# Weight transposes at other places in a queue of tile transposes, one tile's statistics sooner, and another order of V tiles and fusion groups

## The chip, the cores and the metric

The kernel runs on one core of a Trainium2 chip. The metric is the device time of one execution in microseconds; below it is the median of three runs. All times in the text are microseconds, and times inside an execution count from the start of its span.

## The reference

x has 2048 rows (tokens) of 640 values in bf16. Each row is normalised (mean and variance over its 640 values), and the result xn feeds two branches. Their sum and x itself make the output.

- Branch A is linear attention with 32 heads of 20 values. q, k, v = xn @ wqkv. A small matrix per head (w_phi, 20 x 20) turns q and k into features: softmax(p) and softmax(-p) side by side, p = q w_phi or k w_phi. Per head kv = sum over tokens of phi_k v, z = sum over tokens of phi_k; the output is (phi_q kv) / (phi_q z + 1e-6), then @ wo.
- Branch B is a gated unit with 1536 hidden values: (silu(xn w1) * (xn w3)) @ w2.

```python
xn = _layernorm(x)
return x + _A_ref(xn, A_wqkv, A_w_phi, A_wo) + _B_ref(xn, B_w1, B_w3, B_w2)
```

## The kernel before

The rows are cut into 16 tiles of 128 tokens. TensorE contracts over the partition dimension, so it wants xn transposed: xnT holds 5 chunks of 128 of the 640 values, by token. All of the program's order is written out by hand (a manual schedule): within an engine, instructions run in the order in which the text emits them, and engines wait for each other by semaphores.

The work has three stages. The first, which the change touches, normalises and transposes all 16 tiles, computes v of all tiles, and folds w_phi into the weights of k. The second makes phi_k tile by tile and accumulates kv, with units of the gated branch between. The third makes phi_q, the quotient and the two output products tile by tile.

The pieces of the first stage, by the names that the text uses:

- `ld_tiles(t, n)` (lines 128 to 132) loads n tiles of x, `ld_glu(f0, f1)` (114) columns of w1 and w3. All DMAs are issued by SyncE (SP), one after the other, and their data run on the same 16 DMA engines.
- `stats(t, n)` (563) takes the statistics of n tiles: bn_stats and bn_aggr on VectorE (203, 204), then the inverse square root by a short chain on GpSimd (212 to 242).
- `lx(t, n)` (570) normalises the tiles in place, on VectorE (255) or, for tiles 12 and 13, on ScalarE (250).
- `T(t)` (260) transposes a normalised tile into xnT. Tiles 0 to 3 go over TensorE. From tile 4 on it is a DMA transpose from SBUF to SBUF, issued by SP (265).
- `ldT(wkT, 1, d)` (120 to 124) is a DMA transpose of rows 128 d to 128 d + 127 of k's weights out of DRAM, 128 x 640 values. There are five pieces. The text calls them K0 to K4. The five of q's weights follow them.
- `V(t)` (300) is v of tile t: ten matmuls of 128 x 320 (290) that read xnT of the tile, and two copies from PSUM to SBUF on ScalarE (303).
- `FB(d)` (580) is one fusion group: six small matmuls that multiply piece Kd by the block-diagonal w_phi (371), and two copies of the result into wkphi[:, d] on ScalarE (380). It needs Kd.
- `unit()` (588) is a unit of the gated branch for tokens 0 to 511, five matmuls of gate and five of up (387); calling what it returns (g0() to g4()) makes the product on VectorE (400, 403).
- `phi_blocks()` (361) builds the block-diagonal w_phi on VectorE.

The stage ends with `V(12), FB(0), FB(1), V(13), FB(2), FB(3), V(14), FB(4), V(15)` (672). The second stage starts with the product pk of tile 0 (`by_token`, 283 to 298): it goes over the five chunks c = 0 to 4 with two matmuls each, and chunk c reads wkphi[:, c].

PSUM has six banks of one kind, taken in turn, two by each V and by each odd FB; an even FB takes a pair of its own.

Of the kernel before, what the change touches and what calls it, by code (L numbers as in the profile page):

```python
# [12 lines left out]
def kernel(  # L13
# [55 lines left out]
    def bank(name, dt=f32):  # L69
        n = 512 if dt == f32 else 1024  # L70
        return psum.tile([P, n], dt, name=name, tag="bank")

    def pair(name):
        return psum2.tile([P, 2, 512], f32, name=name, tag="pair")
# [21 lines left out]
    wkT, wqT, wv = w_nat[:, 0], w_nat[:, 1], w_nat[:, 2]  # L96
# [11 lines left out]
    def ld(dst, src):  # L108
        nc.sync.dma_start(out=dst, in_=src)
# [4 lines left out]
    def ld_glu(f0, f1):  # L114
        for w, src in ((w1, B_w1), (w3, B_w3)):
            ld(w[:, :, f0:f1], src[:, f0:f1].rearrange("(c p) f -> p c f", p=P))

    wps = one.tile([P, KD, Dh], bf, name="wps")
    with tc.manual_schedule():
        def ldT(dst, i, d):  # L120
            rows = slice(d * P, (d + 1) * P)
            nc.sync.dma_start_transpose(  # L122
                out=dst[:, :, rows], in_=A_wqkv[rows, i * D : (i + 1) * D]
            )
# [3 lines left out]
        def ld_tiles(t, n):  # L128
            ld(
                xin[:, (t // 4) % 3, t % 4 : t % 4 + n],  # L130
                x2[t * P : (t + n) * P, :].rearrange("(t p) d -> p t d", p=P),
            )
# [66 lines left out]
        def ln_stats(t):  # L199
            xt = xin[:, (t // 4) % 3, t % 4, :]  # L200
            st = work.tile([P, 2, 6], f32, name="st")
            for i in range(2):
                nc.vector.bn_stats(out=st[:, i, :], in_=xt[:, i * HD : (i + 1) * HD])  # L203
            nc.vector.bn_aggr(out=mv[:, t, :], in_=st[:])
# [5 lines left out]
        def ln_pow(t, n):  # L210
            r = slice(t, t + n)
            nc.gpsimd.tensor_scalar(
                out=ve[:, r], in0=mv[:, r, 1], scalar1=EPS, scalar2=None, op0=ALU.add
            )
            nc.gpsimd.tensor_tensor(out=ry[:, r], in0=ve[:, r], in1=mhalf[:, 0:n], op=ALU.pow)  # L215

        def ln_newton(t, n):


            r = slice(t, t + n)  # L220
            eng = nc.vector if t < BY_DMA else nc.gpsimd
            if n == 1:
                eng.tensor_scalar(
                    out=rstd[:, r], in0=ry[:, r], scalar1=ve[:, r], scalar2=ry[:, r],
                    op0=ALU.mult, op1=ALU.mult,
                )
            else:
                eng.tensor_mul(out=rstd[:, r], in0=ry[:, r], in1=ry[:, r])
                eng.tensor_mul(out=rstd[:, r], in0=rstd[:, r], in1=ve[:, r])
            if t < BY_DMA:  # L230
                nc.vector.scalar_tensor_tensor(
                    out=rstd[:, r], in0=rstd[:, r], scalar=-3.0, in1=ry[:, r],
                    op0=ALU.add, op1=ALU.mult,
                )
            else:
                nc.gpsimd.tensor_scalar(
                    out=rstd[:, r], in0=rstd[:, r], scalar1=-0.5, scalar2=1.5,
                    op0=ALU.mult, op1=ALU.add,
                )
                nc.gpsimd.tensor_mul(out=rstd[:, r], in0=rstd[:, r], in1=ry[:, r])  # L240
            if t in BY_ACT:
                nc.gpsimd.tensor_scalar(
                    out=shift[:, r], in0=mv[:, r, 0], scalar1=rstd[:, r], scalar2=-1.0,
                    op0=ALU.mult, op1=ALU.mult,
                )

        def ln_x(t):
            xt = xin[:, (t // 4) % 3, t % 4, :]
            if t in BY_ACT:
                nc.scalar.activation(  # L250
                    out=xt, in_=xt, func=AF.Identity,
                    scale=rstd[:, t : t + 1], bias=shift[:, t : t + 1],
                )
                return
            nc.vector.tensor_scalar(  # L255
                out=xt, in0=xt, scalar1=mv[:, t, 0:1], scalar2=rstd[:, t : t + 1],
                op0=ALU.subtract, op1=ALU.mult,
            )
# [102 lines left out]
        def phi_blocks():  # L361
            nc.vector.tensor_mul(
                out=wphi[:],
                in0=wps[:, :, None, :].to_broadcast([P, KD, 8, Dh]),
                in1=mask[:, :, :, None].to_broadcast([P, KD, 8, Dh]),
            )

        def fuse(dst, wT, d, ps):

            for b, c, h0, h1 in PARTS:  # L370
                nc.tensor.matmul(  # L371
                    ps[b][:, Dh * (h0 - 16 * b) : Dh * (h1 - 16 * b)],
                    wT[:, c, d * P : (d + 1) * P],
                    wphi[:, c, h0 - 6 * c : h1 - 6 * c, :],
                    start=((b, c) in ((0, 0), (1, 2))),
                    stop=((b, c) in ((0, 2), (1, 4))),
                    skip_group_check=True,
                )
            for b in range(2):
                nc.scalar.copy(out=dst[:, d, b * HD : (b + 1) * HD], in_=ps[b][:, 0:HD])  # L380
# [182 lines left out]
        def stats(t0, n):  # L563
            for t in range(t0, t0 + n):
                ln_stats(t)
            ln_pow(t0, n)
            if t0 >= BY_DMA:
                ln_newton(t0, n)

        def lx(t0, n):  # L570
            if t0 < BY_DMA:
                ln_newton(t0, n)
            for t in range(t0, t0 + n):
                ln_x(t)
# [3 lines left out]
        T, V = x_transposed, v_unit  # L578

        def FB(d):  # L580
            if d % 2:
                ps = [bank("pf"), bank("pf")]
            else:
                both = pair("pf")
                ps = [both[:, 0], both[:, 1]]
            fuse(wkphi, wkT, d, ps)

        def unit():
            return glu_unit(*glu.pop(0))
# [25 lines left out]
        T(3)  # L615
        ld_tiles(12, 2)
        ld_tiles(14, 2)
        V(2)
        V(3)
        stats(4, 2)  # L620
# [5 lines left out]
        g0()  # L626
        lx(6, 2)
        T(6, 7)
        ldT(wkT, 1, 0)
        stats(8, 1)  # L630
        stats(9, 1)
        g2 = unit()
# [7 lines left out]
        lx(9, 1)  # L640
        T(9)
        ld_glu(512, 768)
        ldT(wkT, 1, 1)
        V(7)
        stats(10, 2)
        g3 = unit()
        stats(12, 1)
        lx(10, 2)
        T(10, 11)
        ldT(wkT, 1, 2)  # L650
        stats(13, 1)
        V(8)
        g3()
        stats(14, 2)
        lx(12, 1)
        T(12)
        V(9)
        ldT(wkT, 1, 3)
        g4 = unit()
        lx(13, 1)  # L660
        T(13)
        V(10)
        ldT(wkT, 1, 4)
        phi_blocks()
        g4()
        lx(14, 2)
        T(14, 15)
        V(11)
        ld_glu(768, F)
        for d in range(KD):  # L670
            ldT(wqT, 0, d)
        V(12), FB(0), FB(1), V(13), FB(2), FB(3), V(14), FB(4), V(15)


        acc = pair("pkv")
# [105 lines left out]
```

## Time and profile before

| | |
|---|---|
| median of 3 runs | 273.03 (272.68 to 273.33) |
| the profiled execution | 273.45 |
| its span, first to last instruction | 271.6 |
| TensorE busy | 263.9 (97% of the span) |
| VectorE, ScalarE, GpSimd busy | 189.9, 109.6, 97.1 |
| granted TensorE clock | 1.0 throughout |

The span is what the profile shows; some 1.85 of the execution lie outside it. Busy times of matmuls are modelled: a matmul's shown length holds a tail in which the next one already runs, so two matmuls in a row overlap in the view. A row of the timeline merges equal instructions that follow each other; its first number is the start of the first one. "SPq" rows are DMAs being issued, and the length is the time for which the issue held SyncE, not the transfer. The DMA view has the time from issue to landing.

### The profile page before, as it was taken

To read this page: it belongs to the slowest core of one execution; us is meant where nothing else is said; L and a number is where in the kernel's file an instruction comes from. 1 tells how busy PE (TensorE), PEld (TensorE's weight loads), DVE (VectorE), ACT (ScalarE), POOL (GpSimd) and SP (SyncE) were. 2 spreads that over 40 slices of the span, in tenths; PEclk is the share of its full clock that TensorE was granted. 3 is DMA by queue.
4 is the path that set the end of the run, shared out by engine and by line. 5 is a ranking of instruction groups with operands and counts; after the bars stand their busy time and mean duration, and the time that the engine had idled before them with its cause. 6 is when DMAs were issued, how large, how long until landed. Compare 5 with 4: busy or idle time off the path is not lost.

```text
span 271.6 us, 5174 instructions
## 1 busy us (share of the span) xinstructions
PE 263.9 (97%) x1972; PEld 166.7 (61%) x1990; DVE 189.9 (70%) x349; ACT 109.6 (40%) x258; POOL 97.1 (36%) x104
## 2 busy tenths in 40 slices
PE   7899989999999999999999999999999999999995
PEld 7646566555555555555554455677777777777773
DVE  5999740887766777777778778877676677777341
ACT  6734657534555553455564455422222222221000
POOL 5254630454333333344433312333334444433000
PEclk9999999999999999999999999999999999999999
DMA  6997858950000000000000944346775765576931
GB/s 209 321 202 140 189 116 236 200 138 0 2 0 2 0 0 2 0 5 0 0 2 5 279 113 77 78 107 143 120 162 129 135 143 126 126 137 142 148 102 54
DMA packets 64380, 27.80 MB, mean 102 GB/s; under 512 B 50144, under 2 KB 64352, under 8 KB 64352
## 3 DMA queue, kind: packets, MB, share of 16 engines
q1 hardware_dynamic: 64352, 27.43, 45.6%
q8 instruction: 17, 0.28, 0.4%
q14 instruction: 11, 0.09, 0.1%
HBM read 12.81 MB, written 2.62 MB: 57 GB/s over the span
## 4 chain that ended last, share of the span: by engine, by line
PE 92%; DVE 2%; DMA 2%; SPq 1%; issue 1%; POOL 1%; ACT 0%
PE acc L505 27%; PE up L387 19%; PE gp L387 19%; PE pq L290 8%; PE pk L290 8%; PE pv L290 6%; PE pkv L413 2%; PE pr L442 2%; DVE st L203 1%; DMA xnT<-reg_h 1%; DMA reg_h<-in_A_x_dram 1%; PE pf L371 1%; SPq L122 0%; POOL ry L215 0%; DVE reg_h L255 0%
## 5 line engine op out<-in xcount | busy, mean ns | idle before, releaser
L353 POOL TENSOR_TENSOR phi<-phi,rk 128x1320 bf16<-128x1320 bf16 x32 | 77.2, 2412 | 136.8 <-DVE rk L352 132.8
L350 DVE TENSOR_REDUCE sk<-phi 128x66 f32<-128x1320 bf16 x32 | 48.9, 1528 | 41.7 <-ACT phi L317 40.7
L387 PEld LDWEIGHTS <-w 128*128 128x128 bf16 x480 | 45.5, 98 | 50.6
L387 PE MATMUL up<-xnT,w 128*128 128x512 bf16 x237 | 59.5, 379 | 0.3
L290 PEld LDWEIGHTS <-xnT 128*128 128x128 bf16 x480 | 45.4, 98 | 23.0 <-DMA xnT<-reg_h 2.4
L387 PE MATMUL gp<-xnT,w 128*128 128x512 bf16 x225 | 58.5, 378 | 0.7
L505 PE MATMUL acc<-reg_v,reg_h 128*128 128x320 bf16 (+2 forms) x384 | 54.9, 299 | 0.0
L317 ACT ACTIVATE phi<-pq 128x360 bf16<-128x360 f32 (+1 forms) x64 | 23.3, 451 | 59.2 <-POOL phi L353 53.8
L505 PEld LDWEIGHTS <-reg_h 128*128 128x128 bf16 x384 | 37.3, 98 | 14.4
L395 ACT ACTIVATE th<-gp 128x512 f32<-128x512 f32 x48 | 28.8, 600 | 34.6 <-PE gp L387 30.6
L403 DVE SCALAR_TENSOR_TENSOR reg_h<-gs,up 128x512 bf16<-128x512 bf16 x48 | 33.0, 688 | 5.3 <-PE up L387 0.5
L317 ACT ACTIVATE phi<-pk 128x360 bf16<-128x360 f32 (+1 forms) x64 | 23.3, 451 | 24.7 <-PE pk L290 15.7
L400 DVE SCALAR_TENSOR_TENSOR gs<-th,gp 128x512 bf16<-128x512 f32 x48 | 31.6, 658 | 0.0
L514 DVE TENSOR_TENSOR res<-acc,xr 128x320 bf16<-128x320 f32 (+2 forms) x32 | 14.3, 487 | 21.5 <-PE acc L505 21.5
L290 PE MATMUL pk<-wkphi,xnT 128*128 128x360 bf16 (+2 forms) x160 | 24.6, 300 | 0.0
L290 PE MATMUL pq<-wqphi,xnT 128*128 128x360 bf16 (+2 forms) x160 | 24.6, 299 | 0.0
L505 PE MATMUL acc<-reg_w,reg_v 128*128 128x320 bf16 (+2 forms) x160 | 24.5, 299 | 0.0
L290 PE MATMUL pv<-reg_w,xnT 128*128 128x320 bf16 x160 | 23.2, 299 | 1.3 <-DMA xnT<-reg_h 1.3
L352 DVE RECIPROCAL rk<-sk 128x66 f32<-128x66 f32 x32 | 18.1, 566 | 3.2
L505 PEld LDWEIGHTS <-reg_v 128*128 128x128 bf16 x160 | 15.7, 98 | 6.1
L303 ACT CAST reg_v<-pv 128x320 bf16<-128x320 f32 x32 | 12.1, 430 | 11.4 <-PE pv L290 11.4
L203 DVE BATCH_NORM_STATS2 st<-reg_h 128x6 f32<-128x320 bf16 x32 | 13.7, 469 | 2.1 <-DMA reg_h<-in_A_x_dram 2.1
(62 smaller groups left out, 135.2 us busy)
## 6 DMA issues: line engine op xcount, KB each, us to landing
xr<-in_A_x_dram SPq DMA_DIRECT2D x16, 160.0 KB, 2.5
out_dram<-res SPq DMA_DIRECT2D x15, 160.0 KB, 1.8
reg_h<-in_A_x_dram SPq DMA_DIRECT2D x7, 320.0 KB, 5.8
w<-in_B_w_dram SPq DMA_DIRECT2D x6, 320.0 KB, 5.7
w<-in_B_w_dram SPq DMA_DIRECT2D x2, 960.0 KB, 6.8
reg_v<-in_B_w_dram SPq DMA_DIRECT2D x3, 640.0 KB, 6.1
reg_w<-in_A_wo_dram SPq DMA_DIRECT2D x1, 800.0 KB, 6.3
reg_w<-in_A_wqkv_dram SPq DMA_DIRECT2D x2, 320.0 KB, 4.5
```

What stands on the lines that cost most here:

```text
L203: nc.vector.bn_stats(out=st[:, i, :], in_=xt[:, i * HD : (i + 1) * HD])
L290: nc.tensor.matmul(ps[i][:, 0 : b - a], xnT[:, c, cols], w[:, c, a:b], start=(c == 0), stop=(c == KD - 1), skip_group_check=True,)
L317: nc.scalar.activation(out=to[g], in_=p.rearrange("p (c f) -> p c f", f=60), func=AF.Exp, scale=1.0 - 2.0 * g,)
L350: nc.vector.reduce_sum(out=sk[:], in_=rows, axis=AX.X)
L352: nc.vector.reciprocal(out=rk[:], in_=sk[:])
L353: nc.gpsimd.tensor_mul(out=rows, in0=rows, in1=rk[:, :, :, None].to_broadcast([P, 2 * NCH, 3, Dh]))
L387: nc.tensor.matmul(ps[:], w[:, c, fi * P : (fi + 1) * P], xnT[:, c, sc * 512 : (sc + 1) * 512], start=(c == 0), stop=(c == KD - 1),)
L395: nc.scalar.activation(out=th[:], in_=gp[:], func=AF.Tanh, scale=0.5)
L400: nc.vector.scalar_tensor_tensor(out=gs[:], in0=th[:], scalar=1.0, in1=gp[:], op0=ALU.add, op1=ALU.mult)
L403: nc.vector.scalar_tensor_tensor(out=hT[:, 4 * sc : 4 * sc + 4, fi, :], in0=gs[:].rearrange("p (t s) -> p t s", t=4), scalar=0.5, in1=up[: ...
L505: nc.tensor.matmul(ps[:, 0 : b - a], rows[j][0], rows[j][1][:, a:b], start=(j == 0), stop=(j == len(rows) - 1),)
L514: nc.vector.tensor_tensor(out=res[:, a:b], in0=ps[:, 0 : b - a], in1=xr[:, a:b], op=ALU.add)
```

## The change

Four of the five K pieces are issued at other places among the tile transposes. SP's order, from the loads of tiles 12 to 15 on:

| | |
|---|---|
| before | T4 T5 T6 T7 K0 T8 T9 w(512:768) K1 T10 T11 K2 T12 K3 T13 K4 T14 T15 w(768:1536) |
| after | K0 T4 T5 T6 T7 K1 T8 T9 w(512:768) K2 T10 T11 T12 T13 K3 T14 T15 K4 w(768:1536) |

The statistics of tile 13 stand ahead of the normalisation of tiles 10 and 11 (VectorE's order changes in this one place; GpSimd's order is the same). At the end of the stage, FB(3) and V(14) change places, and FB(4) and V(15). ScalarE's copies follow the order of the groups that they empty. Nothing is added or left out.

```diff
         ld_tiles(14, 2)
+        ldT(wkT, 1, 0)
         V(2)
...
         T(6, 7)
-        ldT(wkT, 1, 0)
+        ldT(wkT, 1, 1)
...
         ld_glu(512, 768)
-        ldT(wkT, 1, 1)
+        ldT(wkT, 1, 2)
         V(7)
         stats(10, 2)
         g3 = unit()
         stats(12, 1)
+        stats(13, 1)
         lx(10, 2)
         T(10, 11)
-        ldT(wkT, 1, 2)
-        stats(13, 1)
         V(8)
...
         V(9)
-        ldT(wkT, 1, 3)
         g4 = unit()
         lx(13, 1)
         T(13)
+        ldT(wkT, 1, 3)
         V(10)
-        ldT(wkT, 1, 4)
         phi_blocks()
         g4()
         lx(14, 2)
         T(14, 15)
+        ldT(wkT, 1, 4)
         V(11)
...
-        V(12), FB(0), FB(1), V(13), FB(2), FB(3), V(14), FB(4), V(15)
+        V(12), FB(0), FB(1), V(13), FB(2), V(14), FB(3), V(15), FB(4)
```

## The prediction

> **What bounds the kernel now.** I read the busy shares first, then TensorE's instructions in order of time around the moved lines, then SyncE's own order, then single transfers from issue to landing.
>
> ```profile
> PE 263.9 (97%) x1972; PEld 166.7 (61%) x1990; DVE 189.9 (70%) x349; ACT 109.6 (40%) x258; POOL 97.1 (36%) x104
> ```
>
> TensorE is busy 97% of the span, and its order is fixed. So the change is worth what it takes from, or adds to, the moments in which TensorE stands still. The timeline of TensorE where the order was changed (start, length, line, operation, count, and in brackets idle time and what ended it):
>
> ```profile
> 32.38 1.24 PE L387 MATMUL up<-xnT,w 128*128 128x512 bf16 x5
> 33.46 2.88 PE L290 MATMUL pv<-reg_w,xnT 128*128 128x320 bf16 x20
> 36.59 1.53 PE L290 MATMUL pv<-reg_w,xnT 128*128 128x320 bf16 x10 [0.24 <-DMA xnT<-reg_h]
> 37.95 0.79 PE L371 MATMUL pf<-wphi,reg_w 128*128 128x140 bf16 x12
> 39.24 1.53 PE L290 MATMUL pv<-reg_w,xnT 128*128 128x320 bf16 x10 [0.49 <-DMA xnT<-reg_h]
> 40.61 0.79 PE L371 MATMUL pf<-wphi,reg_w 128*128 128x140 bf16 x12
> 41.95 1.53 PE L290 MATMUL pv<-reg_w,xnT 128*128 128x320 bf16 x10 [0.55 <-DMA xnT<-reg_h]
> 43.32 0.48 PE L371 MATMUL pf<-wphi,reg_w 128*128 128x140 bf16 x6
> 43.64 1.52 PE L290 MATMUL pv<-reg_w,xnT 128*128 128x320 bf16 x10
> 44.99 0.44 PE L290 MATMUL pk<-wkphi,xnT 128*128 128x360 bf16 x2
> ```
>
> These are V(10)+V(11), V(12), FB(0)+FB(1), V(13), FB(2)+FB(3), V(14), FB(4), V(15), and the first pk. The lengths hold a tail that overlaps the next matmul, so I count from start to start. An undisturbed V takes 1.36 (36.59 to 37.95; twice that is 2.72), an FB 0.32 (43.32 to 43.64). V(12) could have started at 33.46 + 2.72 = 36.18 and starts at 36.59: 0.41 lost. V(13) could have started at 37.95 + 0.64 = 38.59: 0.65 lost. V(14) at 40.61 + 0.64 = 41.25: 0.70 lost. Together **1.76 us**, more than the 1.28 in the brackets, since those leave out the tails. All three wait for a DMA transpose. Why they come so late stands in SyncE's order:
>
> ```profile
> 31.69 2.15 SPq L122 DMA_TRANSPOSE reg_w<-in_A_wqkv_dram  x1
> 33.94 1.23 SPq L265 DMA_TRANSPOSE xnT<-reg_h  x1
> 35.22 1.27 SPq L122 DMA_TRANSPOSE reg_w<-in_A_wqkv_dram  x1
> 36.59 1.23 SPq L265 DMA_TRANSPOSE xnT<-reg_h  x1
> 37.87 1.27 SPq L122 DMA_TRANSPOSE reg_w<-in_A_wqkv_dram  x1
> 39.23 2.55 SPq L265 DMA_TRANSPOSE xnT<-reg_h  x2
> 41.83 1.14 SPq L109 DMA_DIRECT2D w<-in_B_w_dram  x2
> ```
>
> K2, T(12), K3, T(13), K4, T(14)+T(15), then weights, almost without a pause. Every transpose holds SyncE for 1.23 to 1.27 us, and a quiet one lands 2.6 us after its issue:
>
> ```profile
> xnT<-reg_h SPq DMA_TRANSPOSE x1, 2.6
> ```
>
> 33.94 + 2.6 is V(12)'s start, 36.59 + 2.6 is V(13)'s, and 39.23 + 2.7 V(14)'s. So here SyncE's queue, not the data, sets the pace: one V and two FB are 2.00 us of TensorE's work, one T and one K are 2.50 us of SyncE's.
>
> **The change part by part.** *K2 to K4 later or earlier in the queue.* The three stalls go if each T has landed when TensorE wants it. That depends on the other end of the move: the same five K pieces must be issued somewhere, and the first now stands ahead of T(4). What happens there:
>
> ```profile
> 18.70 1.24 PE L387 MATMUL gp<-xnT,w 128*128 128x512 bf16 x5
> 19.78 1.24 PE L387 MATMUL up<-xnT,w 128*128 128x512 bf16 x5
> 20.98 0.31 PE L290 MATMUL pv<-reg_w,xnT 128*128 128x320 bf16 x1
> ```
>
> TensorE is through with g2 at 19.78 + 1.08 = 20.86 and starts V(4) at 20.98. The transposes around it, behind the last load ahead of them, each issue with its time to landing (T(4), T(5), T(6), T(7), K0):
>
> ```profile
> 14.54 0.41 SPq L109 DMA_DIRECT2D reg_h<-in_A_x_dram  x1
> 16.08 2.02 SPq L265 DMA_TRANSPOSE xnT<-reg_h  x1
> xnT<-reg_h SPq DMA_TRANSPOSE x1, 4.9
> 18.21 1.21 SPq L265 DMA_TRANSPOSE xnT<-reg_h  x1
> xnT<-reg_h SPq DMA_TRANSPOSE x1, 3.5
> 19.51 1.23 SPq L265 DMA_TRANSPOSE xnT<-reg_h  x1
> xnT<-reg_h SPq DMA_TRANSPOSE x1, 2.7
> 20.83 1.23 SPq L265 DMA_TRANSPOSE xnT<-reg_h  x1
> xnT<-reg_h SPq DMA_TRANSPOSE x1, 3.4
> 22.11 1.27 SPq L122 DMA_TRANSPOSE reg_w<-in_A_wqkv_dram  x1
> reg_w<-in_A_wqkv_dram SPq DMA_TRANSPOSE x1, 3.8
> ```
>
> T(4) lands at 16.08 + 4.9 = 20.98, just when V(4) starts: V(4) waits for it already, only 0.12 us. T(4) is slow for the loads ahead of it. From 18.5 to 19.5 us the DMA view has this:
>
> ```profile
> q1 hardware_dynamic: 20, 0.02, 6.6%
> ```
>
> 20 packets, 6.6% of 16 engines: one engine is still emptying its share of the earlier loads while the other fifteen stand. A transpose has a share on each engine, so T(4) ends only when the last engine has come to it. A K piece issued before T(4) lies in front of it on that engine too. **I expect K0 to take T(4)'s place, T(4) that of T(5), and so on**: K0 lands near 21, T(4) at 18.21 + 3.5 = 21.71, T(5) at 19.51 + 2.7 = 22.21, T(6) at 20.83 + 3.4 = 24.23, T(7) at 22.11 + 3.8 = 25.91 or sooner, since a T is shorter than a K. The earlier issue (14.95, behind the load, instead of 16.08) gains nothing, because the engine that is late is late by the loads. V(4) then starts 21.71 - 20.98 = **0.73 us later**. V(5), V(6) and V(7) are wanted at 23.07, 24.43 and 25.79: covered, the last one barely. Bounds for this price: nothing, if the pieces pass side by side, and 18.21 - 16.08 = 2.13, if T(4) is held on SyncE for a place as long as that of the first transpose. Below nothing is excluded: a transfer put ahead of T(4) in its own queue cannot bring it sooner. I take 0.73, the spacing of two transposes in this very place. The Trainium skill, "DMA: Bandwidth & Descriptors", section "Latency and other measured facts", gives a DMA transpose 261 GB/s; 128 x 640 two-byte values would take 0.63 us by it, an estimate, and the sum below would come out 0.10 lower; the trace's 0.73 agrees within that.
>
> *The same stretch after the change.* SyncE: K0 to about 18.1, T(4) to T(7) to 23.3, K1, T(8), T(9), weights, K2, T(10), T(11) at 1.23 to 1.27 each (weights 1.14) to 32.4, with no pause. T(12) then goes at 32.4 instead of 33.94. K2 held SyncE for 2.15 in that place; if T(12) is held as long, it ends at 34.6. T(13) ends at 35.8, K3 at 37.1, T(14) at 38.4, T(15) at 39.7, K4 at 41.0. TensorE, 0.73 later, wants V(12) at 36.91, V(13) at 36.91 + 1.36 + 0.64 = 38.91, V(14) at 38.91 + 1.36 + 0.32 = 40.59, V(15) at 42.27 and FB(4) at 43.63. A T lands about 1.4 us after its issue ends (2.6 - 1.23): T(12) at 36.0, T(13) at 37.2, T(14) at 39.8, T(15) at 41.1, K4 near 42.7. All in time, by 0.8 us or more. The **1.76 us go**.
>
> *Statistics of tile 13 sooner.* They are put ahead of the normalisation of tiles 10 and 11, on which T(10) hangs:
>
> ```profile
> 28.55 0.80 DVE L255 TENSOR_SCALAR reg_h<-reg_h,mv,rstd 128x640 bf16<-128x640 bf16 x2 [1.26 <-POOL rstd L240]
> 29.26 0.88 DVE L203 BATCH_NORM_STATS2 st<-reg_h 128x6 f32<-128x320 bf16 x2
> ```
>
> VectorE idles 1.26 us there, waiting for GpSimd. Tile 13's statistics, in the old order the second row, are 0.88 and one short aggregation; they fit in, so this is hidden. Were that cover gone, T(10) would move by about 0.9 and the aggregation. The other end of the move, tile 13's normalisation on ScalarE, is
>
> ```profile
> 33.18 0.92 ACT L250 ACTIVATE reg_h<-reg_h,shift,rstd 128x640 bf16<-128x640 bf16 x1
> ```
>
> and done at 34.10, ahead of T(13)'s new place at 34.6. Tiles 14 and 15 are ready, even at their old time, at
>
> ```profile
> 36.63 0.80 DVE L255 TENSOR_SCALAR reg_h<-reg_h,mv,rstd 128x640 bf16<-128x640 bf16 x2 [0.63 <-POOL rstd L240]
> ```
>
> 37.43; T(14) would then be issued 0.3 later and land at 40.1, still ahead of 40.59. I cost this part at nothing.
>
> *FB(4) last.* In the old order V(15) covered the two copies of FB(4)'s result. Now the first pk stands right behind FB(4). Its first eight matmuls read pieces 0 to 3 and its last two read piece 4, which must be copied:
>
> ```profile
> 44.02 0.78 ACT L380 CAST wkphi<-pf 128x320 bf16<-128x320 f32 x2
> ```
>
> Two copies take 0.78. V(15)'s two, of the same shape, come first: from 43.7, just after V(15) ends at 43.63, four copies end at 43.7 + 1.56 = 45.26. Without a stall pk would start at 44.99 - 1.76 + 0.73 = 43.96 and reach piece 4 at 43.96 + 8 x 0.136 = 45.05. A stall of **0.2**; bounds nothing (the copies overlap) and 1.3 (pk waits from its start).
>
> *Sum:* -1.76 + 0.73 + 0.2 = **-0.83 us**. The profiled execution took 273.45 with a span of 271.6, and is 0.42 above the median of the runs shown (273.03). Taken off the median: **272.2 us**. Behind the first pk TensorE is at work all the way to the end, so the shift should last. The late columns of w1 and w3 are issued last in both orders and move with the queue.
>
> **The rivals.** *K0 costs nothing.* T(4) lands as before, and only 0.2 stands against 1.76: -1.56, 271.5 us. For it speaks that SyncE stood idle from 14.95 to 16.08; against it, the late engine. The Trainium skill, same page, "Rules for kernel authors", advises to issue a DMA early so that its fixed setup cost lies beside compute; by that rule this rival would come out. The 4.9 us of T(4) speak against it: in this place time passes in a queue, not in setup.
>
> *The waits come back later.* T(12) now stands where K2 stood, and K2 was slow in both issue and landing:
>
> ```profile
> reg_w<-in_A_wqkv_dram SPq DMA_TRANSPOSE x1, 4.2
> ```
>
> At 4.2 from 32.4 T(12) lands at 36.6, only 0.3 ahead of V(12). If T(10) to T(12) run another microsecond late, one of V(10) to V(12) waits some 0.6 to 0.7: about -0.2 in all, 272.8 us, no change that can be told.
>
> *K0 holds T(4) for a whole place of the slow kind.* This is the slower side. If K0 is issued in 2.02 or more and T(4) behind it is held as long again, T(4) comes 2.13 late, and T(5) to T(7) with it: -1.76 + 2.13 + 0.2 = +0.6, 273.6 us. If the piece of K, read from memory beside the loads, is slower than a T, it is more, to some 274. It decides from a delay of 1.56; at 2.1 it is slower beyond what can be told. For it speaks that the very first transpose was slow and that K pieces landed in 3.8 to 4.2 beside loads; against it, that T(5), second in line, was issued in 1.21.
>
> **How the numbers follow.** About 0.2% (0.55 us) is what a measurement can tell from no change. Chances: forecast 0.48 (272.2; its own range 271.9 to 272.5), K0 free 0.08, waits come back 0.22, whole slow place 0.22. Faster by over 0.2% are the first two, 0.56; within, 0.22; slower, 0.22. The range reaches from the free K0 to the middle of the slower case: 271.4 to 273.8.
>
> **What would show it.** V(4) at about 21.7 with T(4) landing there: the price. V(12), V(13), V(14) without a DMA in their brackets, and pk at about 44.0 instead of 44.99: the gain. A wait of 0.1 to 0.3 inside the first pk: the copies. T(10) issued near 29.8, with VectorE's normalisation of tiles 10 and 11 still at 28.55: the statistics are free. The prediction is wrong if T(4) lands after 22.5, if V(5) to V(11) show a wait for a DMA, or if later stages take up the shift.

## The result, and the profile after

The changed kernel takes 272.4 us (median of 21 runs, 271.99 to 273.43) against 273.03 (median of 21 runs beside them, 272.63 to 273.55). The ratio is 0.9981, with a 95% interval of 0.9972 to 0.9990: faster, by 0.3 to 0.8 us. 272.2 was forecast. The profiled execution took 272.0 us. Its busy shares:

```profile
span 270.3 us, 5192 instructions
...
PE 263.7 (98%) x1990; PEld 165.9 (61%) x1990; DVE 189.8 (70%) x349; ACT 109.6 (41%) x258; POOL 97.1 (36%) x104
```

The span is 1.3 us shorter, TensorE's busy time the same. The two profiles differ more than the medians do, because the first execution lies 0.42 above its median and the second 0.4 below its own: 1.45 - 0.82 = 0.63, the difference of the medians. TensorE's timeline in the changed kernel, from unit g2 to the first unit of the second stage:

```profile
19.64 1.24 PE L387 MATMUL up<-xnT,w 128*128 128x512 bf16 x5
20.72 5.60 PE L290 MATMUL pv<-reg_w,xnT 128*128 128x320 bf16 x40
...
32.11 1.24 PE L387 MATMUL up<-xnT,w 128*128 128x512 bf16 x5
33.82 4.25 PE L290 MATMUL pv<-reg_w,xnT 128*128 128x320 bf16 x30 [0.47 <-DMA xnT<-reg_h]
37.90 0.79 PE L371 MATMUL pf<-wphi,reg_w 128*128 128x140 bf16 x12
38.54 1.52 PE L290 MATMUL pv<-reg_w,xnT 128*128 128x320 bf16 x10
...
43.56 1.65 PE L290 MATMUL pk<-wkphi,xnT 128*128 128x360 bf16 x10
45.04 1.24 PE L387 MATMUL gp<-xnT,w 128*128 128x512 bf16 x5
```

Count from start to start again. V(4) starts at 19.64 + 1.08 = 20.72, with no wait at all. V(10) could have started at 32.11 + 1.08 = 33.19 and starts at 33.82: **0.63 lost, a new wait**. From there to the first pk nothing is lost: V(10) to V(12), two FB and V(13) follow each other, and no bracket is left. From the end of g2 to the first pk it is 43.56 - 20.72 = 22.84; before it was 44.99 - 20.86 = 24.13. The difference of 1.29 is the three old waits (1.76) and V(4)'s 0.12, less the new 0.63, within 0.04. The first pk lasts 1.48 to the next gate; before it was 1.38:

```profile
46.37 1.24 PE L387 MATMUL gp<-xnT,w 128*128 128x512 bf16 x4
```

(46.37 - 44.99, from the profile of before.) SyncE's order of the changed kernel, K0 and T(4) to T(7), then T(10) to T(13), K3, T(14)+T(15), K4, weights:

```profile
14.99 1.73 SPq L122 DMA_TRANSPOSE reg_w<-in_A_wqkv_dram  x1
16.82 5.18 SPq L265 DMA_TRANSPOSE xnT<-reg_h  x4
...
28.90 6.89 SPq L265 DMA_TRANSPOSE xnT<-reg_h  x4
35.84 1.27 SPq L122 DMA_TRANSPOSE reg_w<-in_A_wqkv_dram  x1
37.20 2.56 SPq L265 DMA_TRANSPOSE xnT<-reg_h  x2
39.81 1.27 SPq L122 DMA_TRANSPOSE reg_w<-in_A_wqkv_dram  x1
41.14 1.15 SPq L109 DMA_DIRECT2D w<-in_B_w_dram  x2
```

All five K pieces stand at another place than before, not four. From T(13) on the times are the forecast ones: T(13) ends at 35.79 (35.8 was worked out), K3 at 37.11 (37.1), T(15) at 39.76 (39.7), K4 at 41.08 (41.0). They are reached by another path. T(10) to T(12), and the normalisation of tile 13 on ScalarE, which T(13) needs:

```profile
28.90 4.34 SPq L265 DMA_TRANSPOSE xnT<-reg_h  x3
33.65 0.92 ACT L250 ACTIVATE reg_h<-reg_h,shift,rstd 128x640 bf16<-128x640 bf16 x1 [0.68 <-POOL shift L242]
```

T(12) lets SyncE go at 33.24 and not at 34.6. SyncE then stands idle for 1.35 and issues T(13) at 34.59, just behind the end of the normalisation at 34.57. So here T(13) waits for its tile and not for the queue, which costs nothing: it lands at 37.2, and V(13) starts at 38.54. K0 held SyncE for 1.73 only, to 16.72 and not to 18.1. Why V(10) waits is seen in the DMA view of 31.6 to 33.8 us, in 40 slices:

```profile
DMA  9999999999999000000000100000000010039999
...
q8 instruction: 1, 0.02, 3.1%
```

A packet of 16 KB of instructions starts on one DMA engine near 31.7 (1 packet, 3.1% of 16 engines in 2.2 us, so some 1.1 us on one). From about 32.3 to 33.5 the engines then move next to nothing, in the midst of T(10). From 32.5 to 33.3 the data queue has this:

```profile
q1 hardware_dynamic: 18, 0.00, 5.6%
```

5.6% of 16 engines is a little less than one engine: one comes late to its share of the transpose, and the others stand. These 18 packets begin near 32.8, when the 1.1 us of the instruction packet are over. T(10), issued at 28.90, has this row:

```profile
xnT<-reg_h SPq DMA_TRANSPOSE x1, 4.9
```

It lands at 33.8, when V(10) starts.

### The profile page after: what moved, and what is told of

Same layout as the page of the kernel before. It is cut to its first block, busy times and chain, and to the rows that moved or that the text cites. A ratio compares the mean times of both kernels' runs of the same rounds, so it can differ in the third digit from the quotient of the medians.

```text
span 270.3 us, 5192 instructions
## 1 busy us (share of the span) xinstructions
PE 263.7 (98%) x1990; PEld 165.9 (61%) x1990; DVE 189.8 (70%) x349; ACT 109.6 (41%) x258; POOL 97.1 (36%) x104
## 4 chain that ended last, share of the span: by engine, by line
PE 87%; DVE 5%; POOL 3%; DMA 3%; issue 1%; ACT 0%; DVEq 0%
PE acc L505 27%; PE gp L387 17%; PE up L387 17%; PE pq L290 8%; PE pk L290 8%; PE pv L290 4%; DVE st L203 2%; PE pkv L413 2%; PE pr L442 2%; DMA xnT<-reg_h 2%; POOL ry L215 1%; PE pf L371 1%; DVE reg_h L255 1%; DMA reg_h<-in_A_x_dram 1%; DVE mv L204 1%
## 5 line engine op out<-in xcount | busy, mean ns | idle before, releaser
L387 PE MATMUL gp<-xnT,w 128*128 128x512 bf16 x240 | 59.6, 379 | 0.0
L505 PEld LDWEIGHTS <-reg_h 128*128 128x128 bf16 x384 | 37.3, 98 | 14.5
L400 DVE SCALAR_TENSOR_TENSOR gs<-th,gp 128x512 bf16<-128x512 f32 x48 | 31.6, 659 | 0.0
L352 DVE RECIPROCAL rk<-sk 128x66 f32<-128x66 f32 x32 | 18.1, 566 | 3.2
```

The source lines that it names most:

```text
L352: nc.vector.reciprocal(out=rk[:], in_=sk[:])
L387: nc.tensor.matmul(ps[:], w[:, c, fi * P : (fi + 1) * P], xnT[:, c, sc * 512 : (sc + 1) * 512], start=(c == 0), stop=(c == KD - 1),)
L400: nc.vector.scalar_tensor_tensor(out=gs[:], in0=th[:], scalar=1.0, in1=gp[:], op0=ALU.add, op1=ALU.mult)
L505: nc.tensor.matmul(ps[:, 0 : b - a], rows[j][0], rows[j][1][:, a:b], start=(j == 0), stop=(j == len(rows) - 1),)
```

## The experiments

Two theories were set against each other. The **queue theory** is that of the prediction: the order of the transposes on SyncE, against the moments at which TensorE wants them, sets the waits. The **chance theory** is that the moment at which an instruction transfer falls among the transposes sets them. Eleven runs followed, two of them second runs of the change and of the kernel before, each timed in five rounds beside the kernel before. The ratio is to the kernel before. The last row rests on 6 executions, the others on 11 or 12.

| kernel | median us | ratio, 95% interval |
|---|---|---|
| the change, again | 272.65 | 0.9978 (0.9964 to 0.9991) |
| the change, K0 behind T(7) | 272.83 | 0.9987 (0.9973 to 1.0001) |
| the change, K2 behind T(12) | 273.09 | 0.9992 (0.9977 to 1.0007) |
| the change, FB(4)'s copies on VectorE | 272.31 | 0.9975 (0.9963 to 0.9988) |
| before, again | 272.99 | 0.9999 (0.9983 to 1.0014) |
| before, new order of V and FB | 273.53 | 1.0018 (1.0005 to 1.0031) |
| the change, K pieces alone | 272.85 | 0.9992 (0.9981 to 1.0002) |
| the change, columns 512 to 767 sooner | 272.45 | 0.9984 (0.9972 to 0.9995) |
| before, statistics of tile 13 sooner | 273.27 | 0.9999 (0.9987 to 1.0010) |
| the change, last load in halves | 272.78 | 0.9985 (0.9973 to 0.9996) |
| the change with three edits | 272.36 | 0.9967 (0.9955 to 0.9979) |

**The change, again.**

> The changed kernel once more, for a second profile. Queue theory (the order of the DMA transposes on SyncE against TensorE's wants decides; the gain is the three waits ahead of V(12), V(13), V(14), part of it paid back ahead of V(10) and in the first pk): the same places again, first pk at 43.5 to 43.8, V(4) without a wait, V(10) with 0.4 to 0.7, time 272.4 within 0.3. Rival, chance theory (where the 16 KB instruction transfers fall among the transposes decides, and the first profile was a lucky one, with one at 13.3 instead of 15.2): the transfers lie elsewhere, V(4) waits up to 0.7, first pk at 44 or later.

The timeline of TensorE in this second profile, V(10) and unit g6 of the second stage:

```profile
34.11 4.25 PE L290 MATMUL pv<-reg_w,xnT 128*128 128x320 bf16 x30 [0.40 <-DMA xnT<-reg_h]
...
48.86 1.24 PE L387 MATMUL gp<-xnT,w 128*128 128x512 bf16 x5
50.25 1.25 PE L387 MATMUL up<-xnT,w 128*128 128x512 bf16 x5
```

The time is as expected. V(4) again starts without a wait (21.08, right behind g2), V(10) again loses 0.57 (its g4 ends at 33.54), and the first pk is at 43.84. A place that was not looked for shows up: g6's up could have started at 48.86 + 1.08 = 49.94 and starts at 50.25. It waits 0.31 for the last load of w3, which was issued at 42.28 and landed 7.9 later. In the first profile of the change it does not wait.

**K0 behind T(7).**

```diff
         ld_tiles(14, 2)
-        ldT(wkT, 1, 0)
...
         T(6, 7)
+        ldT(wkT, 1, 0)
         ldT(wkT, 1, 1)
```

> The changed kernel with K0 issued behind T(7), directly ahead of K1, instead of ahead of T(4). Queue theory as predicted (K0 ahead of T(4) costs 0.73): T(4) lands 0.6 to 0.7 sooner, and the time falls by 0.4 to 0.7 wherever V(4) waits in the changed kernel. If V(4) waits for nothing in it, as its first profile has it (T(4) landed 20.65, V(4) started 20.72): T(4) lands near 20.0, V(4) starts at the same 20.7, time within 0.2 of the changed kernel. A slower time by more than 0.2 would mean that the early K0 is itself a gain.

T(4) is issued at 16.30 instead of 16.82 and lands at 19.8, about 0.8 sooner than in the profile of the change. V(4) starts no sooner for it: right behind g2, as there. So K0's price is there as a landing time, and nobody waits for it. What comes later is this, T(10) to T(13) on SyncE and V(10) to V(12) on TensorE:

```profile
30.15 6.00 SPq L265 DMA_TRANSPOSE xnT<-reg_h  x4
```

```profile
35.05 4.25 PE L290 MATMUL pv<-reg_w,xnT 128*128 128x320 bf16 x30 [1.27 <-DMA xnT<-reg_h]
```

With one more piece between T(7) and T(10), T(10) is issued 1.25 later and V(10) waits 1.44 from start to start, more than twice as long. The median is 0.18 above that of the change, not more than the 0.2 that was to count as a gain from the early K0, and the intervals overlap. So the early K0 does not cost 0.73 in the timed runs. In this profile it is part of the gain: in the change it uses a time in which SyncE stood idle.

**K2 behind T(12).**

```diff
         ld_glu(512, 768)
-        ldT(wkT, 1, 2)
...
         T(12)
+        ldT(wkT, 1, 2)
```

> The changed kernel with K2 issued between T(12) and T(13), where SyncE stands idle for 1.35 us, instead of ahead of T(10). Queue theory: T(10) has one transpose fewer ahead of it and lands before 33.2, the 0.63 wait of V(10) goes, the first pk starts near 43.0, 0.5 to 0.6 faster than the changed kernel (271.8). Chance theory: the instruction transfer near 31.7 holds whatever transpose is in flight, so V(11) or V(12) waits instead and the time stays within 0.2.

TensorE's timeline, V(10) to V(12), V(14), and g6's up:

```profile
33.30 4.24 PE L290 MATMUL pv<-reg_w,xnT 128*128 128x320 bf16 x30
...
40.54 1.53 PE L290 MATMUL pv<-reg_w,xnT 128*128 128x320 bf16 x10 [0.70 <-DMA xnT<-reg_h]
...
50.42 1.25 PE L387 MATMUL up<-xnT,w 128*128 128x512 bf16 x5 [0.27 <-DMA w<-in_B_w_dram]
```

V(10)'s wait goes, as the queue theory had it. But T(12) held SyncE long, the gap was gone, and K2 pushed T(13) and T(14) back: V(14) waits 0.86 from start to start, and g6's up 0.43 for the last load. The time is 0.4 above the change: both forecasts missed. The waits are those of a fuller queue (K2 ends at 35.05, and T(13) is issued at 35.15 instead of 34.59). Why T(12) held SyncE for 1.92, against 1.58 in the change, is not shown; an instruction packet started near 31.3 here too.

**FB(4)'s copies on VectorE.**

```diff
+                if d == 4 and wT is wkT:
+                    nc.vector.tensor_copy(
+                        out=dst[:, d, b * HD : (b + 1) * HD], in_=ps[b][:, 0:HD]
+                    )
+                    continue
                 nc.scalar.copy(out=dst[:, d, b * HD : (b + 1) * HD], in_=ps[b][:, 0:HD])
```

> The changed kernel with FB(4)'s two copies on VectorE, which is idle there, instead of ScalarE behind V(15)'s copies. If the first pk waits for these copies: its length from start to the next gp falls from 1.48 to 1.38, 0.1 us faster. If it does not: no change.

```profile
43.62 1.57 PE L290 MATMUL pk<-wkphi,xnT 128*128 128x360 bf16 x10
45.03 1.24 PE L392 MATMUL gp<-xnT,w 128*128 128x512 bf16 x5
```

From the first pk to the next gate it is 1.41 instead of 1.48. So the copies were the wait, and most of it goes. The medians, 272.31 and 272.65 for the change, with overlapping intervals, cannot show a difference of 0.07.

**Before, again.**

> The kernel before once more, for a second profile. Its first profile had V(4) 0.12 late and the three waits ahead of V(12), V(13), V(14) at 0.41, 0.65, 0.70, and its 273.45 us lies 0.42 above the median. Queue theory: the three waits are there again, since SyncE's order sets them, but smaller, 1.2 to 1.5 in all, which would bring the loss at the first pk down to what the medians show; T(4) lands where the loads let it, 20.0 to 21. Chance theory: the waits move with the instruction transfers and at least one of the three is gone.

The waits of TensorE from 10 to 60 us:

```profile
PE pv L290 <- DMA xnT<-reg_h: 1.4, 3, 0.5
```

The same three waits: 0.50, 0.67 and 0.65 from start to start, and 0.27 between V(10) and V(11), 2.1 in all. The queue theory had expected them smaller, 1.2 to 1.5, and they are not; the chance theory had at least one of them gone, and none is. But both profiled executions of the kernel before are slower than their medians, by 0.42 and by 0.70. So what an execution at the median loses at these places no profile shows. V(4) did not wait: T(4) was issued at 16.05 and landed 4.1 later, at 20.1, while V(4) was wanted at 20.83. **The first profile's T(4), landing at 20.98, was a late one.** How late T(4) is goes with an instruction packet ahead of it. In the five profiles with no K piece between the loads and T(4), the packet starts near 14.1, 14.2, 14.5, 14.8 and 15.2, and T(4) takes 3.5, 4.1, 4.1, 4.4 and 4.9 to land.

**The order of V and FB alone.**

```diff
-        V(12), FB(0), FB(1), V(13), FB(2), FB(3), V(14), FB(4), V(15)
+        V(12), FB(0), FB(1), V(13), FB(2), V(14), FB(3), V(15), FB(4)
```

> The kernel before with only the new order V(12), FB(0), FB(1), V(13), FB(2), V(14), FB(3), V(15), FB(4). T(14) still stands behind K4, so V(14) starts no sooner, and FB(3), which stood beside its wait, comes behind it, as FB(4) comes behind V(15): queue theory expects 0.3 to 0.4 slower than the kernel before (one FB of 0.32 and 0.1 for the copies in the first pk), 273.4. A rival that gives the gain to the new order expects 272.4.

FB(2) and V(14):

```profile
40.14 0.48 PE L371 MATMUL pf<-wphi,reg_w 128*128 128x140 bf16 x6
41.49 1.53 PE L290 MATMUL pv<-reg_w,xnT 128*128 128x320 bf16 x10 [0.87 <-DMA xnT<-reg_h]
```

V(14) was wanted at 40.14 + 0.32 = 40.46 and waits 1.03 for T(14). The time is 0.5 us above the kernel before, clear of the interval, as expected. The new order alone is a loss. In its one profile the first pk starts at 44.85, not late, since K2 held SyncE for 1.27 there and not for 2.15 or more as in the other three profiles of the old queue: T(12) is issued at 33.09 instead of 33.94, and V(12) is only 0.13 late. How often that happens in the timed runs of the kernel before is open.

**The K pieces alone.** The K pieces as in the change; the order of V and FB and the statistics as before.

> The changed kernel with the old order V(14), FB(4), V(15) and FB(3) ahead of V(14), and tile 13's statistics at their old place: only the K pieces moved. Queue theory: V(12), V(13), V(14) start without a wait as in the changed kernel, but FB(4) is wanted near 41.9 and K4 lands near 42.8: a wait of 0.8 to 0.9 ahead of FB(4), none for copies in the first pk, so 0.7 to 0.8 slower than the changed kernel, 273.2, about as the kernel before. If the statistics matter, T(13) or T(14) is late as well. Rival: K moves alone give the gain, 272.5.

V(10) to V(12), and FB(4):

```profile
33.46 4.24 PE L290 MATMUL pv<-reg_w,xnT 128*128 128x320 bf16 x30
...
42.85 0.49 PE L371 MATMUL pf<-wphi,reg_w 128*128 128x140 bf16 x6 [1.18 <-DMA reg_w<-in_A_wqkv_dram]
```

V(12) to V(14) start on time and FB(4) waits for K4, as expected, but for 1.33 and not for 0.8 to 0.9. By the ratios the time is only 0.3 to 0.4 above that of the change, not 0.7. In the profile the 1.33 are offset in part: V(10) does not wait (0.6), and pk has no copies to wait for (0.1). The intervals of this kernel and of the change overlap, so that the K pieces alone gain less is likely and not settled. The new order alone loses, and with K4 behind T(15) the old order has FB(4) wait.

This profile also bears on the chance theory. T(10) is issued at 29.15, 0.25 later than in the change, and lands in 3.5 instead of 4.9. The instruction packet is not in the DMA view from 31.6 to 32.6 but from 32.6 to 32.8, when T(10) is through; in the change it was there from 31.6 to 31.8. Taken over all thirteen profiles:

| packet starts, after T(10)'s issue | profiles | T(10) lands after | V(10) waits |
|---|---|---|---|
| 2.5 to 2.8 | 7 | 4.5 to 4.9 | 0.16 to 1.44 |
| 3.2 to 3.5 | 4 | 3.3 to 3.5 | not at all |
| 2.3 to 2.4 | 2 | 2.7 and 2.8 | not at all |

The seven are the change twice, K0 behind T(7), the copies on VectorE, the columns sooner, the load in halves, and, with the old queue, the statistics alone. The last two, K2 behind T(12) and the three edits, have less ahead of T(10); why T(10) escapes the packet there is not shown. No run moves the packet by itself, so this is an agreement of times and not a test. But for this one wait the chance theory fits, and the wait is not one of the changed queue alone.

**Columns 512 to 767 sooner.**

```diff
         T(6, 7)
+        ld_glu(512, 768)
         ldT(wkT, 1, 1)
...
         T(9)
-        ld_glu(512, 768)
```

> The changed kernel with columns 512 to 767 of w1 and w3 loaded behind T(7) instead of behind T(9). In the changed kernel T(10) is issued at 28.9, as soon as its tile is normalised, but its data lie behind these loads (landed at 31.2) and K2, and then the instruction transfer near 31.7 catches it. Queue theory: with the loads gone by then T(10) lands near 31.5 to 32, V(10) starts without a wait, T(8) and T(9) land 1 later and still in time, 0.5 to 0.6 faster than the changed kernel (271.9). Chance theory: the instruction transfer holds T(11) instead and V(11) waits as long; no gain. If T(8) comes late, V(8) waits and the time is that of the changed kernel or above.

The first pk moves to 43.34, but T(10) lands at 33.5 all the same, with the instruction packet in the window from 31.4 to 31.6: so the loads were not what held it, and the packet fits. Then g6:

```profile
48.36 1.24 PE L387 MATMUL gp<-xnT,w 128*128 128x512 bf16 x5
49.73 1.25 PE L387 MATMUL up<-xnT,w 128*128 128x512 bf16 x5
```

Its up waits 49.73 - 49.44 = 0.29 for the last load. The median is no better than the change's: a miss. In the profile, what was won ahead of pk (0.2) is paid back at g6.

**The statistics alone.**

```diff
         stats(12, 1)
+        stats(13, 1)
         lx(10, 2)
...
-        stats(13, 1)
```

> The kernel before with only tile 13's statistics moved ahead of the normalisation of tiles 10 and 11. Queue theory: VectorE idles there, T(10) is issued when it was, T(12) to T(14) are held by SyncE's queue and not by their tiles, so the time is that of the kernel before within 0.2 and the three waits stay at 1.7 to 2.1. Rival (the statistics bring T(14) sooner): V(14)'s wait shrinks by 0.3 or more.

The waits of TensorE from 10 to 60 us:

```profile
PE pv L290 <- DMA xnT<-reg_h: 1.3, 3, 0.8
```

The ratio is 0.9999: nothing, as forecast. T(12), T(13) and T(14) are issued at 33.94, 36.58 and 39.22, as before. From start to start V(10) waits 0.37, V(12) 1.01 and V(14) 0.40, 1.8 in all. V(14)'s wait is 0.3 shorter, the rival's sign, but T(14) comes no sooner: TensorE is later there, because V(10) and V(12) wait longer. So the sum stays, and how it is shared out differs between executions.

**The last load in halves.**

```diff
-        ld_glu(768, F)
+        ld_glu(768, 1152)
+        ld_glu(1152, F)
```

> The changed kernel with the last load of w1 and w3 (columns 768 to 1535) cut in two halves of 384 columns each, the first halves of both first. In two of three profiles of the changed order the up product of unit g6 waits 0.1 to 0.3 for the last of these loads, which lands at 49.5 to 50.2. Theory of the new bound (the changed order runs into this load): with the halves g6 has its columns by 48, its up starts right behind its gate, and the median falls by 0.1 to 0.3 against the changed kernel, 272.2. Rival: the loads are only as late as the transposes ahead, and two more issues cost what they bring; no change.

```profile
34.16 4.25 PE L290 MATMUL pv<-reg_w,xnT 128*128 128x320 bf16 x30 [0.82 <-DMA xnT<-reg_h]
...
48.91 1.24 PE L387 MATMUL gp<-xnT,w 128*128 128x512 bf16 x5
49.99 1.24 PE L387 MATMUL up<-xnT,w 128*128 128x512 bf16 x5
```

g6 does not wait (48.91 + 1.08 = 49.99), but its pk came late, at 43.90, so the old load might have done as well here. The ratio shows no gain (0.9985 against 0.9981 and 0.9978 for the change); this stays inconclusive.

**Three edits together.** The change with FB(4)'s copies on VectorE, columns 512 to 767 sooner, and the last load in halves; the diffs are those above.

> The changed kernel with three more edits: the load of columns 512 to 767 behind T(7), FB(4)'s copies on VectorE, and the last load cut in halves. Theory of the new bound: the first pk starts near 43.3 as with the earlier load alone, the pk loses no time to copies (0.07), and g6 does not wait (0.3 with the earlier load alone), so 0.4 to 0.6 faster than the changed kernel, 271.9. Rival: the waits move on to another place (V(8), whose tile then lands last, or a later load) and the time stays at 272.4.

V(4), V(8), and V(10) to V(12):

```profile
20.14 1.24 PE L392 MATMUL up<-xnT,w 128*128 128x512 bf16 x5
21.48 5.61 PE L290 MATMUL pv<-reg_w,xnT 128*128 128x320 bf16 x40
...
29.48 2.89 PE L290 MATMUL pv<-reg_w,xnT 128*128 128x320 bf16 x20 [0.24 <-DMA xnT<-reg_h]
...
34.37 4.24 PE L290 MATMUL pv<-reg_w,xnT 128*128 128x320 bf16 x30
```

In this execution K0 held SyncE for 3.12, T(4) was issued at 17.97 and landed at 21.47, and V(4) waits 0.26 for it: here the price of the early K0 is paid. V(8) waits 0.40, as T(8) now stands behind the moved load. V(10) and g6 wait for nothing, and from the first pk (44.09) to the next gate it is 1.41. The ratio of 0.9967 is the best of all, clear of the kernel before. It lies 0.3 to 0.4 us below the change, but their intervals overlap, it rests on 6 executions, and the two were not timed side by side. So it beats the kernel before; whether it beats the change is not settled.

## Why the prediction was right

The time, the direction and the size are right: 272.2 was forecast, 272.4 measured. The working is right in its main term and wrong in others, and one of its own signs of being wrong came out: no wait was to show at V(5) to V(11), and V(10) waits. By its own steps:

- **The three waits, 1.76.** Right. They go in every profile with the K pieces where the change has them, but for 0.06 at V(14) with the columns sooner. V(14) waits again when K2 is put behind T(12), and the three profiles of the old queue taken later lose 1.6 to 2.1, though not always at the same tiles. That the queue sets them, and not their tiles, is shown by the statistics alone (T(12) to T(14) issued as before, no change in time) and by the new order alone (V(14) waits on behind K4, slower). That SyncE's times from T(13) to K4 came out within 0.1 is luck: T(12) was to hold SyncE for 2.15 and held it for 1.58, and the rest was an idle time in which tile 13 was not yet normalised (34.57, where 34.10 was read off).
- **K0 ahead of T(4), 0.73.** Wrong as a cost. "I expect K0 to take T(4)'s place, T(4) that of T(5)" failed in the change's two profiles: V(4) did not wait. With K0 behind T(7), T(4) lands 0.8 sooner, so the step between two places is about right. Two other things failed. "The earlier issue gains nothing" was wrong: K0 held SyncE to 16.72 and not to 18.1. And the T(4) from which I counted, landing at 20.98, was a late one, in the execution with the latest instruction packet (15.2); in the second profile of before T(4) landed at 20.1, 0.7 ahead of V(4). With K0 ahead of it T(4) lands some 0.1 to 0.6 ahead of V(4) in seven profiles, and in the eighth V(4) waits 0.26. One reading of the working does not hold either: T(7) at 25.91 is called covered, though V(7) was to want it at 25.79.
- **"All in time."** Wrong for T(10), for which I worked out no landing. It was issued at 28.90, sooner than the 29.8 forecast, and took 4.9 to land, where the working counts 2.6 for every T; V(10) lost 0.63 and 0.57 in the change's two profiles. This is what the rival of the waits that come back foresaw (0.6 to 0.7 at one of V(10) to V(12)); I gave it 0.22. Its likely cause, an instruction transfer that holds up the transpose in flight, was not in the argument. It nearly cancels the error at V(4): 0.73 that was not paid against 0.6 that was. The sum is right partly by this luck.
- **FB(4) last, 0.2.** Mis-sized: 0.10 measured, of which 0.07 went with the copies on VectorE.
- **The statistics, nothing.** Right: alone they leave the time as it is, 0.9999.
- **"Behind the first pk the shift should last."** Right in the first profile; in the second one g6's up takes 0.31 back, and up to 0.43 with other edits. The last load of w1 and w3 moved with the queue, as said, by some 0.7, but TensorE's want moved by 1.3. How often g6 waits in the timed runs stays open.

So the change is worth 0.3 to 0.8 us and not the whole 1.76: in the profiles the rest goes to V(10), to the copies ahead of the first pk's end, and in one of two to g6. This account does not close for the medians. The two profiled spans of the kernel before are 271.6 and 272.0, those of the change 270.3 and 270.9, a mean difference of 1.2, twice the 0.5 to 0.6 between the medians; why an execution of the kernel before at the median takes less time than the profiled ones is open.

## What to carry to other kernels

Where transposes are issued one after the other on one queue, write down when each is issued and when TensorE wants it; a piece that is wanted late belongs into a time in which the queue stands idle, ahead of the crowd, and the groups that use it have to move along: with the old order FB(4) waited 1.33 for its piece. Take the slack at such a place from several executions before charging it as a cost: one profile had 0.1 too little of it where others had 0.7. When a wait of 1.8 us is removed, look at once for the next load that TensorE runs into. And when a queue comes out at the forecast times, look whether it was the queue: here SyncE stood idle for 1.35 us just ahead of them.

## What the runs showed of the hardware

One DMA engine that comes late holds up a whole DMA transpose. In the change a 16 KB packet of instructions starts on one engine near 31.7; from about 32.3 to 33.5 the others move next to nothing, and T(10) takes 4.9 us to land, where it took 3.5 in the profile whose packet started near 32.6. The packet starts between 31.3 and 33.0 us in the thirteen profiles of nearly the same program, so T(10) is caught in seven of them and not in the others. A transpose issued right behind the loads also holds SyncE longer: the same K0 did so for 1.33 to 3.12 us, against 1.27 for a K piece in a quiet place.
